# Mixing-matrix products in 64 by 64 tiles of TensorE, and the steps of the kernel in a new order

## The chip, the core and the metric

The kernel runs on one core of one Trainium2 chip. The metric is device microseconds of one execution; a time is the median of several runs. The engines of the core work from queues of their own, in order, and wait for each other through semaphores: PE (TensorE, matrix products), DVE (VectorE), ACT (ScalarE), POOL (GpSimd) and SP (SyncE, which here only issues transfers). Sixteen DMA engines carry what POOL, SP and ACT issue.

## What is computed

Eight batches, each with eight heads, 576 rows and a head size of 64. A small packed query `p` (32 rows a head) attends to `k`, `v`; the result is key and value for the attention of `q`. Then a mixing block works on the heads side by side (512 columns).

```python
def sm_attn(qq, kk, vv):
    s = scale * np.matmul(qq, kk.transpose(0, 1, 3, 2))
    a = np.exp(s - np.max(s, axis=-1, keepdims=True))
    a = a / (np.sum(a, axis=-1, keepdims=True) + 1e-09)
    return np.matmul(a, vv)

p_packed = sm_attn(p, k, v)
x = sm_attn(q, p_packed, p_packed)      # heads put side by side: (8, 576, 512)

wq, wk = x @ w_q, x @ w_k               # (8, 576, 64)
W_tok = scale * np.einsum('bsd,btd->bst', wq, wk)
mixed = np.einsum('bst,btd->bsd', W_tok, x)
out = np.maximum(mixed, 0.0) @ w_out
```

Inputs and output are 32-bit floats, 9.4 MB for each of `q`, `k`, `v` and the output. The products are made in bf16.

## The kernel before

**Steps and their order.** Nothing is planned at run time. The text `ORDER` (lines 13 to 55) lists 521 steps, and the loop at line 600 issues them one by one. `S2.7.1=0,1` is step S2 of batch 7, part 1, into PSUM banks 0 and 1; `@A`, `@V`, `@P` name ACT, DVE or POOL. Each engine takes its own steps in the order of this text, so the text fixes the order within every queue; between engines only data and buffers decide.

**The products, by batch, and the tile of the TensorE array that each uses.** A matmul on R rows and C columns of the array is called R by C here.

- S1 (line 280): packed query times keys, 32 by 32 tiles. X1, TE: exponential on ACT, transposition on DVE.
- PV (313): weights times values, 64 by 64, four tiles of the array in turn. RC, PP, PT: division and transposition on DVE.
- QK (334): 64 by 64; QKE and QD put its result into SBUF.
- S2 (371): scores of `q` against the packed keys, 64 by 128. It needs PT and QV (the transposition of `q`, DVE line 235). X2 is its exponential (ACT), RS and RR the row sums and their reciprocals (DVE), AM the scaling (POOL or DVE, line 403).
- AT (412, 417), WKQ (439, 444), GM (465): 128 by 128. AE, WE, GE take them out of PSUM.
- Y (475): 64 by 64. YE takes it out and scales it.
- **MX (490) and MR (496)**: the product of the small matrix y (weights) with the transposed query side `wkq` (moving). MX makes 512 moving columns at a time, MR the 64 left over from the last chunk. RL, RLF and RLR are the relu on their results.
- OT (538) and OH (578): the relu's result times `w_out`, 128 by 128, 512 columns. OE, OEF, OEH copy it out of PSUM, and ST, STF, STH store it.

WARM (617) are products on a constant that keep TensorE at work early on.

In MX, the loop over `c` picks the half of the rows of the array, `h = halves(c ^ i)`, and bank `c` of two. One matmul has 64 rows, all 128 columns and 512 moving elements. MR has the same weights, over `i` and `h`, with 64 moving elements.

**Transfers.** All loads are issued by POOL's queue: `k`, `v`, `q` of a batch into four buffers each, cast from 32 bits to bf16 on the way (576 KB in SBUF for each; `v` in two halves; `q` of batch 7 in two halves, `LD.q7` and `LD.r7`). Stores go from SP, a few from POOL (`ST.0.8`, `ST.1.4`, `ST.1.8`) and one from ACT. The first step of SP after the start is `HOLD.v7` (line 572): a tiny copy that reads the buffer of `v` of batch 7, so SP's stores wait until that load has landed. SP then issues its stores in order, and a store whose data isn't ready holds up those behind it.

Of the kernel before, what the change touches and what calls it, by code (L numbers as in the profile page):

```python
# [23 lines left out]
PV.2.1 RL.0.1@A RS.1.2@V RS.1.1@V MR.0=2,3 RC.2@V RR.1.2@V AM.1.2@P RR.1.1@V WARM.5=0 PP.2.1@V MX.0.0=0,1 AM.1.1@P
PP.2.0@V PT.2@V AT.1.2=4 LD.k4 AT.1.0=5 RL.0.0@A QK.2=6 RLR.0@A QV.2.2@V AT.1.1=7 AE.1.0@V QKE.2@V S2.2.2=0,1
AE.1.2@A AE.1.1@A QD.1@P X2.2.2@A S2.2.3=2,3 WKQ.1.2=4,5 WKQ.1.1 WKQ.1.0 OT.0.2=6,7 X2.2.3@A WE.1.0@A QD.2@P LD.q3
LD.v4 WE.1.1@V GM.1=0 RS.2.4@V KT.3.2@V RR.2.4@V GE.1@A OT.0.3 Y.1=2,3 YE.1@A OT.0.0=4,5 AM.2.2@V OE.0.1@A
S1.3=0,1,2,3 OT.0.1 X1.3.0@A MX.1.0=6,7 MX.1.1=0,1 AM.2.3@V X1.3.1@A AT.2.3=2 AT.2.2=3 OE.0.0@A TE.3.0@V RL.1.1@A
RL.1.0@A TE.3.1@V AE.2.3@V PV.3.0=4,5 AE.2.2@V PV.3.1 MR.1=2,3 WKQ.2.0=0,1 WKQ.2.1 WKQ.2.2 RC.3@V WE.2.2@A KT.4.2@V
RLR.1@A PP.3.0@V OT.1.2=6,7 PP.3.1@V OT.1.3 OE.1.1@A PT.3@V S1.4=0,1,2,3 OT.1.0=4,5 LD.q4 X1.4.1@A LD.k5 QV.3.2@V  # L30
X1.4.0@A GM.2=6 S2.3.3=2,3 LD.v5 GE.2@V X2.3.3@A TE.4.1@V S2.3.2=6,7 X2.3.2@A LD.q5 Y.2=0,1 OT.1.1 YE.2@V OE.1.0@A
MX.2.0=0,1 RL.2.0@A TE.4.0@V RS.3.4@V MX.2.1=2,3 RL.2.1@A PV.4.0=6,7 RR.3.4@V PV.4.1 QK.3=4 OT.1.4=5 RC.4@V
PP.4.1@V PP.4.0@V OEF.1.4@A QV.4.2@V AM.3.3@P OT.2.0=0,1 PT.4@V QKE.3@A OT.2.1 AT.3.3=2 AM.3.2@P QD.3@P LD.k6
AT.3.2=3 OE.2.0@A AE.3.3@V S2.4.2=6,7 S2.4.3=4,5 X2.4.2@A AE.3.2@A KT.5.2@V QK.4=0 QKE.4@V WKQ.3.1=6,7 WKQ.3.0
WKQ.3.2 LD.v6 X2.4.3@A WE.3.2@A RS.4.4@V S1.5=2,3,4,5 X1.5.1@A X1.5.0@A LD.q6 OT.2.2=0,1 GM.3=6 OT.2.3 QD.4@P
TE.5.1@V GE.3@V MR.2=4,5 TE.5.0@V Y.3=2,3 RR.4.4@V RLR.2@V PV.5.0=6,7 OE.2.1@A PV.5.1 LD.k7 AM.4.3@P YE.3@V
MR.3=4,5 RC.5@V PP.5.1@V RLR.3@A MX.3.1=2,3 RL.3.1@A AM.4.2@P MX.3.0=0,1 OT.3.4=4 RL.3.0@A AT.4.3=5 PP.5.0@V PT.5@V
AT.4.2=2 QV.5.2@V QK.5=3 S2.5.2=6,7 OEF.3.4@A AE.4.3@V AE.4.2@A S2.5.3=0,1 LD.q7 QKE.5@A LD.v7 X2.5.2@A KT.6.2@V
WKQ.4.2=4,5 WKQ.4.0 WKQ.4.1 WE.4.2@V OT.3.0=2,3 X2.5.3@A S1.6=6,7,0,1 X1.6.1@A HA.5@P GM.4=4 X1.6.0@A QD.5@P GE.4@V
OT.3.1 Y.4=4,5 TE.6.1@V LD.r7 YE.4@A RS.5.4@V TE.6.0@V RR.5.4@V OT.3.2=0,1 MX.4.0=6,7 MX.4.1=4,5 OE.3.0@A QV.6.2@V  # L40
PV.6.0=2,3 HOLD.v7 AM.5.3@P AM.5.2@P PV.6.1 OT.3.3 RL.4.0@A RL.4.1@A RC.6@V PP.6.0@V PP.6.1@V ST.0.8@P OE.3.1@A
OT.4.0=6,7 MR.4=4,5 RLR.4@A PT.6@V S2.6.3=2,3 S2.6.2=0,1 X2.6.3@A AT.5.2=4 AT.5.3=5 KT.7.2@V OT.4.1 AE.5.3@V
AE.5.2@A X2.6.2@A ST.1.4@P OE.4.0@A RS.6.4@V RR.6.4@V WKQ.5.2=2,3 WKQ.5.1 WKQ.5.0 AM.6.3@P S1.7=0,1,4,5 WE.5.2@A
# [5 lines left out]
OT.5.1 ST.1.8@P RR.7.0@V OT.5.2=4,5 RR.7.1@V AM.7.2@P ST.5.4 ST.4.1 AM.7.0@V QD.7@P RL.6.1@A RL.6.0@A AT.7.2=6
ST.3.1 AT.7.0=7 AM.7.1@V AE.7.0@V OE.5.0@A AT.7.1=0 AE.7.2@V OT.5.3 WKQ.7.2=6,7 AE.7.1@V WKQ.7.0 WE.7.0@V WKQ.7.1  # L50
OT.6.0=2,3 OE.5.1@A WE.7.1@A GM.7=0 GE.7@V OT.6.1 ST.4.0 Y.7=4,5 OT.6.2=6,7 ST.5.0 YE.7@V MX.7.1=0,1 OE.6.0@A
OEF.6.2@A MX.7.0=4,5 MR.7=2,3 RLF.7.0.1@V RLF.7.0.0@A ST.3.0 ST.5.1 RLF.7.1.1@V OT.6.3 RLF.7.1.0@A OT.7.1=4
OEF.6.3@A OEF.7.1@A OT.7.2=0 OT.7.0=1 RLR.7@A STF.6.2 OH.7.0=2 ST.6.0 OEF.7.2@A STF.6.3 STF.7.1 OEF.7.0@A OT.7.4=3
# [5 lines left out]
def kernel(  # L59
# [426 lines left out]
    def MX(b, i, eng, bk):  # L486
        ps = T["mx", b, i] = bank(bk, [C, 512])
        for c in range(C):
            h = halves(c ^ i)
            nc.tensor.matmul(ps[:, c], T["y", b][h, i], T["wkq", b][h, :, 128:384], start=True, stop=True)  # L490

    def MR(b, eng, bk):
        ps = T["mr", b] = ps_all[:, bk[0]:bk[1] + 1, 0:2 * GR].rearrange("a c (i g) -> a c i g", g=GR)
        for i in range(2):
            for h in range(2):
                nc.tensor.matmul(ps[:, h, i], T["y", b][halves(h), i], T["wkq", b][halves(h), 1, 384:NW],
                                 start=True, stop=True)
# [153 lines left out]
```

## Time and profile before

| | |
|---|---|
| time, median of 3 runs | 104.42 us (104.15 to 104.46) |
| time of the profiled execution | 104.16 us |
| its span (first to last instruction of the program) | 102.3 us |
| PE, DVE, ACT, POOL busy | 91%, 71%, 64%, 47% of the span |
| granted TensorE clock | 1.0 of full speed throughout |
| read from HBM, written to it | 30.15 MB, 9.44 MB |
| issues of SP, POOL, ACT that store results | 18, 3, 1 |

Between the span and the time of the same execution lie 1.86 us that the program's instructions don't cover. Rows of a timeline show the start in us from the beginning of the span, the length, engine, line, operation, output and inputs, sizes and count; in square brackets the idle time before and what ended it. Rows that merge several matmuls give the first start and the time to the last end; an end is modelled and lies some 0.2 us behind the last start, so for the pace of TensorE starts are compared with starts. SPq and POOLq are the queues of SP and POOL.

### The profile page before, as it was taken

To read this page: it belongs to the slowest core of one execution; us is meant where nothing else is said; L and a number is where in the kernel's file an instruction comes from. 1 tells how busy PE (TensorE), PEld (TensorE's weight loads), DVE (VectorE), ACT (ScalarE), POOL (GpSimd) and SP (SyncE) were. 2 spreads that over 40 slices of the span, in tenths; PEclk is the share of its full clock that TensorE was granted. 3 is DMA by queue.
4 is the path that set the end of the run, shared out by engine and by line. 5 is a ranking of instruction groups with operands and counts; after the bars stand their busy time and mean duration, and the time that the engine had idled before them with its cause. 6 is when DMAs were issued, how large, how long until landed. Compare 5 with 4: busy or idle time off the path is not lost.

```text
span 102.3 us, 3572 instructions
## 1 busy us (share of the span) xinstructions
PE 93.1 (91%) x1524; PEld 56.5 (55%) x1540; DVE 72.6 (71%) x145; ACT 65.1 (64%) x109; POOL 48.2 (47%) x78
## 2 busy tenths in 40 slices
...
DMA  1899999999999999999999999999999999998991
GB/s 11 243 225 210 212 213 211 207 210 214 203 214 203 216 206 211 211 213 207 213 214 205 210 213 205 215 212 207 207 267 395 415 425 377 407 415 344 395 382 62
DMA packets 13279, 25.13 MB, mean 246 GB/s; under 512 B 1040, under 2 KB 6416, under 8 KB 13008
## 3 DMA queue, kind: packets, MB, share of 16 engines
...
q8 instruction: 12, 0.20, 0.7%
...
HBM read 30.15 MB, written 9.44 MB: 387 GB/s over the span
## 4 chain that ended last, share of the span: by engine, by line
PE 60%; DMA 23%; DVE 7%; issue 3%; POOL 2%; ACT 1%; DVEq 0%; POOLq 0%
PE ps L538 24%; DMA q_sb<-in_q_dram 23%; PE ps L617 13%; PE ps L313 4%; PE ps L371 3%; PE ps L490 3%; PE ps L417 2%; DVE qT L235 2%; PE ps L444 2%; POOL a L403 2%; PE ps L280 2%; PE ps L465 2%; PE ps L439 2%; PE ps L334 1%; DVE kT L235 1%
## 5 line engine op out<-in xcount | busy, mean ns | idle before, releaser
L538 PE MATMUL ps<-wout,relu 128*128 128x512 bf16 x112 | 29.3, 380 | 0.8 <-issue 0.3
L403 POOL TENSOR_TENSOR a<-e,rr 128x256 bf16<-128x256 f32 (+2 forms) x15 | 15.9, 1071 | 25.2 <-DVE rr L397 16.3
L617 PE MATMUL ps<-o 128*128 128x128 f32 (+3 forms) x80 | 22.6, 432 | 1.3 <-DVE o L133 1.2
L126 ACT ACTIVATE o<-ps 128x1024 f32<-128x1024 f32 (+2 forms) x19 | 16.6, 873 | 5.9 <-PE ps L538 4.4
L538 PEld LDWEIGHTS <-relu 128*128 128x128 bf16 x124 | 10.5, 98 | 11.2 <-issue 1.2
L617 PEld LDWEIGHTS ps<-o 128*128 128x128 f32 x80 | 13.2, 230 | 6.1 <-issue 3.9
L501 ACT ACTIVATE relu<-ps 128x1024 bf16<-128x1024 f32 (+1 forms) x15 | 13.9, 971 | 1.5 <-PE ps L490 1.5
L291 ACT ACTIVATE e1T<-ps 128x576 bf16<-128x576 f32 x16 | 9.6, 649 | 7.5 <-PE ps L280 6.9
L235 DVE STREAM_TRANSPOSE kT<-k_sb 128x1152 uint32<-128x1152 uint32 (+1 forms) x9 | 11.2, 1243 | 2.4 <-DMA k_sb<-in_k_dram 2.4
L376 ACT ACTIVATE e<-ps 128x256 f32<-128x256 f32 (+2 forms) x19 | 11.2, 631 | 2.1 <-PE ps L371 1.9
L392 DVE TENSOR_REDUCE rs<-e 128x16 f32<-128x512 f32 (+2 forms) x13 | 11.0, 854 | 1.8 <-ACT e L376 1.8
L235 DVE STREAM_TRANSPOSE qT<-q_sb 128x1152 uint32<-128x1152 uint32 (+1 forms) x10 | 11.1, 1115 | 1.2 <-DMA q_sb<-in_q_dram 1.1
L171 POOL DMA_DIRECT2D v_sb<-in_v_dram x16 | 10.0, 629 | 3.3 <-PE ps L280 1.4
L235 DVE STREAM_TRANSPOSE e<-e1T 128x288 uint32<-128x288 uint32 x16 | 7.3, 465 | 2.3 <-ACT e1T L291 2.1
L313 PE MATMUL ps<-v_sb,e 64*64 64x192 bf16 x288 | 7.8, 245 | 0.3 <-ACT o L126 0.2
L313 PEld LDWEIGHTS <-e 64*64 64x64 bf16 x288 | 6.0, 107 | 2.7 <-DVE e L235 1.4
L444 PE MATMUL ps<-aT,pqk 128*128 128x256 bf16 (+1 forms) x48 | 7.1, 246 | 0.0
L371 PE MATMUL ps<-ppT,qT 64*128 64x64 bf16 x320 | 6.5, 190 | 0.5 <-DVE qT L235 0.3
L371 PEld LDWEIGHTS <-qT 64*128 64x128 bf16 x320 | 5.5, 94 | 2.6 <-DVE qT L235 2.3
L439 PE MATMUL ps<-pqk,aT 128*128 128x64 bf16 x80 | 5.9, 194 | 0.2 <-ACT aT L126 0.2
L130 DVE COPY aT<-ps 128x1024 bf16<-128x1024 bf16 (+1 forms) x9 | 5.0, 553 | 1.2 <-PE ps L417 1.2
L439 PEld LDWEIGHTS <-aT 128*128 128x128 bf16 x80 | 4.7, 98 | 1.7 <-ACT aT L126 0.6
...
## 6 DMA issues: line engine op xcount, KB each, us to landing
...
```

The source lines that it names most:

```text
L126: nc.scalar.activation(o, i, COPY)
L171: nc.gpsimd.dma_start(v_bufs[b % NL][halves(i), 0:7:2], src)
L235: nc.vector.transpose(o, i)
L313: nc.tensor.matmul(T["pv", b][halves(cc), i], lhsT, rhs, start=n == 0, stop=n == R - 1, skip_group_check=True)
L371: nc.tensor.matmul(ps[:, y, t - t0, i], lhsT, rhs, start=e == 0, stop=e == 1)
L376: nc.scalar.activation(e2[:, t0:t1].rearrange("a t (i y n) -> a y (t i) n", i=2, y=2), T["s2", b, c].rearrange("a y t i n -> a y (t i) n") ...
L392: nc.vector.tensor_reduce(rs[:, t0 * H:t1 * H], src, axis=AX, op=ADD)
L403: e.tensor_tensor(a2[:, t0:t1].rearrange("a t i (u l) -> a (t i u) l", l=L), e2v(b, c), T["rr", b][:, t0 * H:t1 * H].to_broadcast((P, (t1 ...
L439: nc.tensor.matmul(o, aT[:, i, t * P:(t + 1) * P], pqk[:, i, 0:Dl], start=i == 0, stop=i == 1)
L501: nc.scalar.activation(o, i, RELU)
L538: nc.tensor.matmul(ps, lhsT, wout[:, j, :], start=j == 0, stop=j == NJ - 1)
L617: nc.tensor.matmul(bank(int(bk), [w]), warm[:, 0:P], rhs, start=True, stop=True)
```

## The change

MX and MR are written with one more loop, over the two halves `z` of the weights' columns. Each matmul becomes two, with 64 columns of weights each, that write to the lower and the upper half of PSUM's partitions. MX has 64 matmuls in place of 32, MR 64 in place of 32.

```diff
     def MX(b, i, eng, bk):
         ps = T["mx", b, i] = bank(bk, [C, 512])
         for c in range(C):
             h = halves(c ^ i)
-            nc.tensor.matmul(ps[:, c], T["y", b][h, i], T["wkq", b][h, :, 128:384], start=True, stop=True)
+            for z in range(2):
+                nc.tensor.matmul(ps[halves(z), c], T["y", b][h, i, halves(z)], T["wkq", b][h, :, 128:384],
+                                 start=True, stop=True)
 
     def MR(b, eng, bk):
         ps = T["mr", b] = ps_all[:, bk[0]:bk[1] + 1, 0:2 * GR].rearrange("a c (i g) -> a c i g", g=GR)
         for i in range(2):
             for h in range(2):
-                nc.tensor.matmul(ps[:, h, i], T["y", b][halves(h), i], T["wkq", b][halves(h), 1, 384:NW],
-                                 start=True, stop=True)
+                for z in range(2):
+                    nc.tensor.matmul(ps[halves(z), h, i], T["y", b][halves(h), i, halves(z)],
+                                     T["wkq", b][halves(h), 1, 384:NW], start=True, stop=True)
```

`ORDER` has the same 521 steps; up to `LD.q2 WKQ.0.1` (in its seventh line) it is unchanged, and behind that the steps stand in another order, 34 of them on another engine. Of the text, the part around the second half of batch 7:

```diff
...
-QD.6@P PP.7.1@V MX.5.0=6,7 RL.5.0@A WKQ.6.2=2,3 PT.7@V WKQ.6.0 WKQ.6.1 WE.6.2@A MX.5.1=4,5 S2.7.1=0,1 OT.5.4=6
-X2.7.1@A GM.6=7 S2.7.2=2,3 RL.5.1@V ST.3.4 GE.6@A X2.7.2@A S2.7.0=0,1 Y.6=4,5 QK.7=7 YE.6@A RS.7.1@V QKE.7@A
...
+AM.6.2@P GE.5@V AT.6.3=0 AT.6.2=1 AE.6.3@V Y.5=6,7 OE.4.1@A PV.7.0=2,3 QV.7.0@V AE.6.2@A YE.5@A PV.7.1 MR.5=4,5
+MX.5.1=0,1 RLR.5@A RC.7@V RL.5.1@A MX.5.0=6,7 WKQ.6.1=4,5 RL.5.0@A WKQ.6.0 WKQ.6.2 PP.7.0@V PP.7.1@V ST.3.0
+OT.5.4=2 PT.7@V S2.7.2=0,1 S2.7.1=6,7 ST.0.8@P WE.6.2@V S2.7.0=4,5 X2.7.2@A RS.7.2@V GM.6=3 GE.6@V OT.5.0=0,1
+OT.5.1 OEF.5.4@A X2.7.0@A RR.7.2@V RS.7.0@V X2.7.1@A Y.6=2,3 RS.7.1@V AM.7.2@P RR.7.0@V AM.7.0@V YE.6@A AT.7.2=4
...
```

What the new text means for the queues, from batch 1 on, read out of it:

```
POOL before: LD.q2 LD.O LD.k3 LD.v3 AM.1.0 AM.1.2 AM.1.1 LD.k4 QD.1 QD.2 LD.q3 LD.v4 LD.q4 LD.k5 LD.v5 LD.q5
             AM.3.3 AM.3.2 QD.3 LD.k6 LD.v6 LD.q6 QD.4 LD.k7 AM.4.3 AM.4.2 LD.q7 LD.v7 HA.5 QD.5 LD.r7
             AM.5.3 AM.5.2 ST.0.8 ST.1.4 AM.6.3 AM.6.2 QD.6 ST.1.8 AM.7.2 QD.7
POOL after:  LD.q2 LD.O LD.k3 LD.v3 LD.k4 AM.1.1 AM.1.2 AM.1.0 QD.1 LD.q3 LD.v4 AM.2.2 AM.2.3 LD.q4 LD.k5 QD.2
             LD.v5 LD.q5 LD.k6 AM.3.3 LD.v6 QD.3 LD.q6 AM.4.2 LD.k7 AM.4.3 LD.v7 LD.q7 QD.4 ST.1.4 HA.5 QD.5
             AM.5.3 AM.5.2 LD.r7 QD.6 AM.6.3 AM.6.2 ST.0.8 AM.7.2 QD.7 ST.1.8
SP before:   HOLD.v7 ST.3.4 ST.2.1 ST.2.0 ST.5.4 ST.4.1 ST.3.1 ST.4.0 ST.5.0 ST.3.0 ST.5.1
             STF.6.2 ST.6.0 STF.6.3 STF.7.1 STF.7.2 STF.7.0 STH.7.0 ST.7.4
SP after:    HOLD.v7 ST.3.0 ST.3.4 ST.2.1 ST.2.0 ST.4.0 ST.5.4 ST.3.1 ST.4.1 ST.5.0 ST.5.1
             ST.6.0 STF.6.2 STF.6.3 ST.7.4 STF.7.1 STF.7.0 STF.7.2 STH.7.0
```

On PE, going through the steps in order and counting every place where the tile shape (32 by 32, 64 by 64, 64 by 128, 128 by 128) differs from that of the step before: 83 places before and 70 after; of these 38 and 33 up to the start of `S2.3.3`, 44 and 36 behind it, one at it. (The old order with the new tiles would have 80, the new order with the old tiles 84.) The last steps on PE are `OT.7.4 OH.7.1` before and `OH.7.1 OH.7.0` after.

More of the change, by code (lines that the diff above doesn't have):

```diff
@@ L24 @@
[L24 to L43, printed above, removed]
@@ L49 @@
[L49 to L53, printed above, removed]
@@ new lines @@
+OE.0.0@A MX.1.0=4,5 AE.2.3@V AE.2.2@A PV.3.0=6,7 LD.v5 MR.1=2,3 PV.3.1 RLR.1@A MX.1.1=0,1 WKQ.2.2=2,3 RL.1.0@V
+RL.1.1@A LD.q5 RC.3@V LD.k6 PP.3.1@V WKQ.2.1 WKQ.2.0 KT.4.2@V PP.3.0@V OT.1.2=4,5 WE.2.2@A OT.1.3 S1.4=0,1,2,3
+OE.1.1@A X1.4.1@A OT.1.0=6,7 PT.3@V X1.4.0@A QV.3.2@V GM.2=4 S2.3.3=2,3 GE.2@V X2.3.3@A TE.4.1@V S2.3.2=0,1 Y.2=4,5
+OT.1.1 YE.2@V X2.3.2@A TE.4.0@V RS.3.4@V MX.2.0=4,5 PV.4.0=2,3 PV.4.1 OE.1.0@A RL.2.0@A RR.3.4@V QK.3=0 RC.4@V
+MX.2.1=6,7 PP.4.1@V OT.1.4=1 PP.4.0@V AM.3.3@P RL.2.1@A OT.2.0=4,5 PT.4@V OT.2.1 AT.3.3=2 QKE.3@A QV.4.2@V
@@ new lines @@
+OEF.1.4@A S2.4.3=6,7 OE.2.0@A X2.4.3@A S2.4.2=0,1 AM.3.2@V LD.v6 QD.3@P AE.3.3@V AT.3.2=3 AE.3.2@A LD.q6 KT.5.2@V
+X2.4.2@A WKQ.3.0=4,5 RS.4.4@V WKQ.3.1 WKQ.3.2 S1.5=6,7,2,3 WE.3.2@A X1.5.0@A OT.2.2=0,1 X1.5.1@A GM.3=4 RR.4.4@V
+AM.4.2@P GE.3@A OT.2.3 Y.3=6,7 TE.5.1@V QK.4=2 TE.5.0@V YE.3@V PV.5.0=4,5 MR.3=6,7 PV.5.1 OE.2.1@A QKE.4@V LD.k7
+AM.4.3@P LD.v7 LD.q7 QV.5.2@V RC.5@V RLR.3@A MR.2=0,1 RLR.2@A MX.3.0=2,3 QD.4@P PP.5.0@V MX.3.1=6,7 OT.3.4=0
+AT.4.3=1 PP.5.1@V PT.5@V AT.4.2=4 RL.3.0@A S2.5.3=2,3 RL.3.1@A OEF.3.4@A S2.5.2=6,7 QK.5=5 AE.4.2@V AE.4.3@V
@@ new lines @@
+WKQ.4.0=0,1 KT.6.2@V WKQ.4.2 QKE.5@V X2.5.3@A WKQ.4.1 OT.3.0=2,3 X2.5.2@A S1.6=6,7,4,5 ST.1.4@P HA.5@P OT.3.1
+QD.5@P X1.6.0@A X1.6.1@A WE.4.2@V RS.5.4@V TE.6.0@V TE.6.1@V GM.4=0 GE.4@A OT.3.2=6,7 HOLD.v7 Y.4=4,5 PV.6.0=0,1
+OE.3.0@A YE.4@A RR.5.4@V PV.6.1 QV.6.2@V MX.4.0=2,3 RC.6@V RL.4.0@A PP.6.1@V AM.5.3@P PP.6.0@V MX.4.1=4,5 RL.4.1@A
+OT.3.3 MR.4=2,3 AT.5.3=0 AM.5.2@P PT.6@V RLR.4@V AT.5.2=1 KT.7.2@V AE.5.2@A S2.6.2=4,5 S2.6.3=2,3 X2.6.2@A QK.6=1
+AE.5.3@V OT.4.0=4,5 X2.6.3@A LD.r7 QKE.6@A RS.6.4@V OE.3.1@A OT.4.1 QD.6@P S1.7=2,3,0,1 OE.4.0@A RR.6.4@V
```

24 lines of the change are left out of this document (16 added, 8 removed).

## The prediction

> **What bounds the kernel now.** I read the page first: shares, slices, and the chain of work that ended last.
>
> ```profile
> span 102.3 us, 3572 instructions
> PE 93.1 (91%) x1524; PEld 56.5 (55%) x1540; DVE 72.6 (71%) x145; ACT 65.1 (64%) x109; POOL 48.2 (47%) x78
> ...
> DMA  1899999999999999999999999999999999998991
> GB/s 11 243 225 210 212 213 211 207 210 214 203 214 203 216 206 211 211 213 207 213 214 205 210 213 205 215 212 207 207 267 395 415 425 377 407 415 344 395 382 62
> ...
> PE 60%; DMA 23%; DVE 7%; issue 3%; POOL 2%; ACT 1%; DVEq 0%; POOLq 0%
> ```
>
> Two things are full at once. TensorE is busy 91% of the span, and the DMA engines show 9 in every slice but two from the second on. The rate has two levels: about 210 GB/s while loads run (they write half of what they read, 32 bits to bf16), and about 400 from slice 30 (76 us) on, when stores run. The chain names PE for 60%, but a chain follows one thread. So I ask where PE waits for data, and whether the DMA engines have anything left to give. First the chain of waits in order of time, then PE's timeline at the same place:
>
> ```profile
> 34.56 11.71 DMA q_sb<-in_q_dram
> ...
> 46.29 1.39 DVE qT L235
> ...
> 47.73 0.78 PE L371 MATMUL ps<-ppT,qT 64*128 64x64 bf16 x40 [0.26 <-DVE qT L235]
> ```
>
> `q` of batch 3 lands at 34.56+11.71 = 46.27, DVE transposes it, and S2.3, for which PE stood idle 0.26 us, begins at 47.73. Up to there PE follows the loads, and time saved on it only lengthens this wait. From there on PE runs behind the loads.
>
> The end of the run, from the busy time in chosen stretches (PE, PEld, DVE, ACT, POOL, then clock, DMA share, GB/s) and SP's queue:
>
> ```profile
> 78.00:80.00 2.00, 2.00 (x50) 1.43 (x43) 1.96 (x6) 1.77 (x5) 1.33 (x3) 1.00 0.96 379
> 85.00:87.00 2.00, 2.00 (x19) 1.17 (x18) 1.54 (x4) 2.00 (x3) 0.01 (x1) 1.00 0.93 370
> 91.00:93.00 2.00, 2.00 (x15) 0.81 (x16) 0.87 (x2) 1.87 (x3) 0.00 (x0) 1.00 1.04 416
> 93.00:95.00 2.00, 2.00 (x11) 0.89 (x10) 0.84 (x2) 1.73 (x5) 0.00 (x0) 1.00 0.84 323
> ```
>
> ```profile
> 76.36 0.60 SPq L572 DMA_DIRECT2D touch<-v_sb  x1
> 77.00 0.58 SPq L557 DMA_DIRECT2D out_dram<-orem  x1
> 77.63 1.51 SPq L561 DMA_DIRECT2D out_dram<-o  x2
> 83.41 0.34 SPq L557 DMA_DIRECT2D out_dram<-orem  x1
> 83.85 6.37 SPq L561 DMA_DIRECT2D out_dram<-o  x6
> 92.61 0.54 SPq L592 DMA_DIRECT2D out_dram<-o  x1
> ...
> 98.37 0.34 SPq L557 DMA_DIRECT2D out_dram<-orem  x1
> ```
>
> With 416 GB/s as the full rate, the stretches at 78, 85 and 93 us lack 0.18, 0.22 and 0.45 us of transfer, 0.85 us in all: (416-379)/416 x 2 and so on. The largest hole, at 93, lies behind SP's pause between 90.2 and 92.61. All else in the tail is full. So whatever PE saves, the end can come forward by about 0.85 us and no more, unless the bytes change, which they don't.
>
> **The change part by part.** *Tile shapes.* What does a change of shape cost? PE's timeline:
>
> ```profile
> 49.59 0.61 PE L490 MATMUL ps<-wkq,y 64*128 64x512 bf16 x4
> 50.12 0.94 PE L313 MATMUL ps<-v_sb,e 64*64 64x192 bf16 x36
> 50.90 0.39 PE L334 MATMUL ps<-wqk,ppT 64*64 64x128 bf16 x8
> ...
> 90.91 1.04 PE L538 MATMUL ps<-wout,relu 128*128 128x512 bf16 x4
> 91.88 0.61 PE L490 MATMUL ps<-wkq,y 64*128 64x512 bf16 x4
> 92.32 0.22 PE L496 MATMUL ps<-wkq,y 64*128 64x64 bf16 x4
> 92.48 3.63 PE L538 MATMUL ps<-wout,relu 128*128 128x512 bf16 x16
> 95.94 0.81 PE L578 MATMUL ps<-wout,relu 128*128 128x384 bf16 x4
> ```
>
> OT's sixteen take 95.94-92.48 = 3.46 us from start to start, 0.216 for 512 columns. MX's four, followed by MR in the same shape, take 92.32-91.88 = 0.44: two rounds of 0.216, two matmuls side by side in each. Followed by PV in another shape, they take 50.12-49.59 = 0.53. The change of shape costs 0.53-0.43 = 0.10 us; between OT and MX it is 0.97-4x0.216 = 0.11. I take 0.10. Behind S2.3.3 the steps change shape 36 times in place of 44: 8 x 0.10 = **0.8 us less on PE**. The five fewer ahead of it lie in front of the wait for `q` and are costed at nothing: that wait hides them, and if it were gone they would give 0.5 more.
>
> *MX itself.* Eight matmuls in place of four for a batch, in two rounds of four tiles. The trace has no 64 by 64 matmul of 512 columns. From below: PV runs four such tiles at once, 36 matmuls in 50.90-50.12 = 0.78 us, of which nine rounds of 192 columns at OT's pace would be 0.73. So MX stays at 0.43: nothing. From above: if the two halves that read the same moving rows ran one after the other, MX would take 0.86, 0.43 more, for six batches (2 to 7) behind S2.3 2.6 us. I take the lower end, PV's row being nearest: same tiles, same type. *MR*: between the 0.06 of now (0.16 from 92.32 to 92.48, less a change of shape) and the 0.18 or so of QK's four rounds (0.39 less the last matmul's 0.2), 0 to 0.7 us for six batches; I take 0, since MR's matmuls have half of QK's columns and its rounds four tiles. *Weight loads*: from the groups of instructions by form,
>
> ```profile
> L490 PEld LDWEIGHTS <-y 64*128 64x128 bf16 x32 | 1.2, 94 | 2.0 <-DVE y L484 0.8 <-issue 0.6 <-ACT y L482 0.4
> L313 PEld LDWEIGHTS <-e 64*64 64x64 bf16 x288 | 6.0, 107 | 2.7 <-DVE e L235 1.4 <-issue 0.4 <-DVE rr L397 0.4
> ...
> L501 ACT ACTIVATE relu<-ps 128x1024 bf16<-128x1024 f32 x13 | 12.8, 1029 | 1.5 <-PE ps L490 1.5
> L503 DVE TENSOR_SCALAR relu<-ps 128x1024 bf16<-128x1024 f32 x1 | 1.2, 1226 | 0.4 <-PE ps L490 0.4
> ...
> L403 POOL TENSOR_TENSOR a<-e,rr 128x1024 bf16<-128x1024 f32 x4 | 7.6, 1904 | 13.9 <-DVE rec L317 7.5 <-DVE rr L397 5.0 <-PE ps L490 1.4
> ```
>
> a load of 64 columns takes 107 ns, longer than one of 128 (94). The 64 loads more lie under the matmuls, as PV's do at full pace: nothing. Uncovered, the eight loads more of a batch would be 0.86 us, 5 us for six batches; PV's pace with a load for every matmul excludes that. The Trainium skill, "TensorEngine Tiling (Array Packing)", Restrictions, speaks against the change here: column tiling switches the fast weight load off. The two durations agree with it; by that rule the loads cost 128 x 107 - 64 x 94 ns = 7.7 us of loading, and by PV's pace none of it shows.
>
> *Engines and the queues of POOL and DVE.* 34 steps change engine, nearly all between ACT and DVE; the longest, a relu of 1024 columns, takes 1.03 us on ACT and 1.23 on DVE, and neither engine is full (64%, 71%). Near the end, OE.5.1 and OE.6.0 go to DVE, which is busy 0.87 of 2 us from 91 to 93. AM.2.2 and AM.2.3 go to POOL, ahead of `LD.q4` and `LD.k5`. POOL's loads have the 11.71 us from issue to landing of the first row above as cover, since several stand in line; the 1.9 us of the larger of them on POOL cost nothing. Without that cover every us late is a us of idle DMA. `LD.k4` and `LD.k6` go earlier, and the order of loads up to `k7` stays.
>
> *SP and the last loads.* Here is the price I do see. Loads come one after another: DVE starts on `q6` at 69.14 and on `k7` at 71.97, both having waited for the landing, so 2.8 us for a full load and 1.4 for half of one. SP's copy at 76.36 marks `v7`'s landing (71.95+1.4+2.8 = 76.2).
>
> ```profile
> 69.14 1.38 DVE L235 STREAM_TRANSPOSE qT<-q_sb 128x1152 uint32<-128x1152 uint32 x1 [0.50 <-DMA q_sb<-in_q_dram]
> 71.97 1.42 DVE L235 STREAM_TRANSPOSE kT<-k_sb 128x1152 uint32<-128x1152 uint32 x1 [0.40 <-DMA k_sb<-in_k_dram]
> ...
> 78.18 0.77 DVE L235 STREAM_TRANSPOSE qT<-q_sb 128x576 uint32<-128x576 uint32 x1
> 79.45 0.15 DVE L317 RECIPROCAL rec<-ps 128x2 f32<-128x2 f32 x1
> 79.64 0.61 DVE L321 SCALAR_TENSOR_TENSOR pp<-ps,rec,mask 128x128 bf16<-128x128 f32 x2
> 80.28 0.31 DVE L235 STREAM_TRANSPOSE ppT<-pp 128x128 uint32<-128x128 uint32 x1
> 80.69 0.40 PE L371 MATMUL ps<-ppT,qT 64*128 64x64 bf16 x16
> ```
>
> Now `v7` is loaded ahead of `q7`, lands at 74.8, and frees SP 1.5 us earlier, while `q7` (76.2), `ST.1.4` (256 KB, 0.6 us: 76.8) and `r7` (78.2) are still to come on POOL's queue. SP's first store, issued at 75.4, has its packets under way by some 77.4: the shortest transfer of the output takes 2.8 us from issue to landing,
>
> ```profile
> DMA to landing us min/median/max: 2.8/5.0/9.6
> ```
>
> of which 0.6 us carries its 256 KB. The last 0.8 us of `r7` then shares the engines and takes 1.6: `r7` at 79.0. QV.7.0 now stands ahead of RC.7, PP.7 and PT.7 on DVE: 0.77+0.15+0.61+0.31 = 1.84, so S2.7 can begin at 80.9 to 81.0. PE would be there at 80.69-0.8+0.87 = 80.8 (OT.5.4, four times 0.216, now comes first). The stall is **0.2 us**, between 0 (no sharing) and 1.2 (sharing from 76.4 on).
>
> *Stores at the end.* `ST.1.8` (1 MB, 2.5 us of transfer) goes from the middle to the end of POOL's queue, behind QD.7, and `ST.3.0` and `ST.4.0` move ahead of the store on which SP waited until 83.41. Both put transfers where holes were (85 and 93 us). PE's last product is followed by a copy of 384 columns in place of 512, 0.1 us shorter, within what I leave uncertain.
>
> *Sum.* 0.8 on PE, less 0.2 at S2.7: 0.6 us, under the 0.85 that the DMA engines allow. Against the execution's own 104.16 that is 103.56; the median of the runs shown lies 0.26 higher, so **103.8 us** on its scale.
>
> **The rivals.**
>
> *Nothing comes out.* The end belongs to the transfers as much as to PE; if the holes of 0.85 us only move (SP waits behind ST.5.4 or ST.5.1 again), the last store lands when it did: 104.4. For it: DMA at 9 throughout. Against: the new order of the stores. The same time follows if the 0.10 us isn't due to the shape but to any change from one step's operands to another's, so that the change doesn't do what it says; MX to MR at 0.44 without it speaks against that.
>
> *Slower: the last load is late.* SP's stores, let go before `q7` and `r7` are in, take half of the engines from 76.4 on (I assume equal shares of two queues); ST.1.4 and `r7` need 1.8 us alone and 3.6 shared, `r7` lands at 80.0, and S2.7 starts at 81.9 to 82.0, 1.2 late. Then 104.42-0.8+1.2 = 104.8; with `q7` caught too or two stores beside each load, 105.2. It decides from a landing of 79.7 on, at which 0.8 are lost. For it: SP's hold is released earlier. Against: issue of the first store at 75.4 needs time to bear. The Trainium skill, "DMA: Bandwidth & Descriptors", Arbitration, has each DMA engine take turns between queues packet by packet; no row of the run before shows it, loads and stores hardly overlapping there.
>
> *Slower: pairs of tiles on the same rows don't overlap.* MX doubles: 104.42-0.6+2.6 = 106.4. PV's and Y's rows speak against it.
>
> **How the numbers follow.** Forecast 0.48, with 103.3 (0.85, the 0.1 of the shorter last copy and half of the 0.26 between profiled time and median) to 104.1 as its own range; no gain 0.20; the late load 0.27; doubled MX 0.05. A measurement of this kernel tells 0.3%, 0.3 us, from no change, so faster means under 104.1: 0.48; within: 0.20; slower: 0.32. The range runs from 103.2 (the same with the whole 0.26) to 105.2 (the late load's far end) and leaves out doubled MX and some of each end.
>
> **What would show it.** MX from start to start at 0.43 for eight matmuls; a change of shape still at 0.10, and 36 of them behind S2.3; S2.3 at 47.7 as before; S2.7 near 81; PE's last product 0.5 to 0.8 us earlier; no stretch under 0.95 of DMA share between 84 and 96. Wrong would be: S2.7 at 82 or later, a slice of DMA under 9 while loads run, or MX at 0.86.

## The result, and the profile after

| | before | changed |
|---|---|---|
| median, 22 runs each | 104.75 us | 105.35 us |
| ratio to before | 1 | 1.0057 (95%: 1.0034 to 1.0081) |
| profiled execution, its span | 104.16, 102.3 us | 104.83, 103.1 us |

The change makes the kernel 0.6 us slower. Runs more than 1.5% above the fastest of the same kernel are left out of every ratio in this document: one of the changed kernel's 22, one each of f1 and h1 below, and five of i2's 12. The forecast was 103.8 us, faster; that was wrong. The median lies just above the range's end of 105.2; on the scale of the prediction's own 104.42 it is 104.42 x 1.0057 = 105.0. From the page of the changed kernel:

```profile
span 103.1 us, 3725 instructions
...
PE 94.7 (92%) x1604; PEld 57.1 (55%) x1604; DVE 75.3 (73%) x147; ACT 62.9 (61%) x106; POOL 50.3 (49%) x79
...
DMA  2999999999999999999999999999989999998974
GB/s 20 236 229 210 213 210 209 210 210 213 206 209 209 210 208 214 210 210 211 209 211 207 217 209 203 216 211 206 226 206 388 402 412 402 393 413 355 366 294 162
...
q8 instruction: 12, 0.20, 0.7%
...
PE 59%; DMA 16%; POOL 7%; ACT 6%; issue 5%; DVE 4%; ACTq 0%; POOLq 0%
```

PE is busy 1.6 us longer, though it has fewer changes of shape to make. The DMA row has an 8 in slice 30 (75 to 77 us), where before has a 9. In the chain of work the share named "issue" has grown from 3% to 5%: time in which PE waited for nothing that the profile shows. PE's timeline, in which the number in square brackets is the idle time ahead of a row:

```profile
48.19 0.78 PE L371 MATMUL ps<-ppT,qT 64*128 64x64 bf16 x40 [0.50 <-ACT e1T L291]
...
50.05 0.41 PE L491 MATMUL ps<-wkq,y 64*64 64x512 bf16 x4
50.29 0.91 PE L313 MATMUL ps<-v_sb,e 64*64 64x192 bf16 x36
...
56.28 0.38 PE L444 MATMUL ps<-aT,pqk 128*128 128x256 bf16 x2
56.96 0.23 PE L439 MATMUL ps<-pqk,aT 128*128 128x64 bf16 x2 [0.29 <-ACT aT L126]
...
64.43 0.29 PE L439 MATMUL ps<-pqk,aT 128*128 128x64 bf16 x4
64.79 0.39 PE L444 MATMUL ps<-aT,pqk 128*128 128x256 bf16 x2
...
66.43 0.48 PE L280 MATMUL ps<-kT,pT 32*32 32x288 bf16 x31
67.09 0.28 PE L280 MATMUL ps<-kT,pT 32*32 32x288 bf16 x1 [0.18 <-issue]
...
70.24 0.60 PE L491 MATMUL ps<-wkq,y 64*64 64x512 bf16 x8
70.78 1.04 PE L541 MATMUL ps<-wout,relu 128*128 128x512 bf16 x4
...
93.47 0.23 PE L499 MATMUL ps<-wkq,y 64*64 64x64 bf16 x8
93.53 0.39 PE L491 MATMUL ps<-wkq,y 64*64 64x512 bf16 x4
```

The tiles do what they were priced at. Four of the new matmuls followed by PV, now in the same shape, take 50.29-50.05 = 0.24; eight with a change of shape behind them take 70.78-70.24 = 0.54, which is 0.44 and 0.10. MR's eight take 0.06. But PE waits in new places: 56.96, 64.79 and 67.09.

To see all of these, I took each matmul's start, less the start before it, less its predecessor's columns at OT's pace, less 0.095 us where the shape changes. What is left is the time lost. Behind S2.3.3, losses over 0.06 us, in us (gaps of 0.216 in OT, which are missing records, are taken off):

```
before   52.60 .08   54.51 .12   56.77 .16   61.33 .12   62.99 .07   65.95 .09   74.01 .16                 sum 0.80
changed  53.07 .19   55.80 .07   56.96 .46   60.21 .19   61.17 .10   61.90 .11   64.79 .24   67.09 .35
         72.67 .12   79.40 .12   81.13 .15   83.33 .08                                                     sum 2.17
```

That is 1.37 us more. S2.3 begins 48.19-47.73 = 0.46 later, and eight changes of shape fewer save 0.76: 1.07 in sum. PE's last matmul starts at 98.89 in place of 97.62, 1.27 later; the other 0.2 isn't attributed. Most of the new loss lies between 53 and 67 us.

The same stretches of the tail as before, with 76 to 78 us added; first the changed kernel, then two rows of before that aren't shown yet:

```profile
76.00:78.00 2.00, 2.00 (x33) 1.31 (x23) 1.79 (x4) 2.00 (x4) 1.15 (x1) 1.00 0.82 224
78.00:80.00 2.00, 2.00 (x48) 1.52 (x49) 1.18 (x3) 1.89 (x5) 1.95 (x3) 1.00 1.03 396
...
85.00:87.00 2.00, 2.00 (x15) 0.67 (x12) 1.96 (x5) 1.02 (x3) 0.35 (x1) 1.00 0.98 388
91.00:93.00 2.00, 2.00 (x28) 0.84 (x24) 1.47 (x2) 0.90 (x3) 0.00 (x0) 1.00 1.03 424
93.00:95.00 2.00, 2.00 (x24) 0.86 (x23) 1.60 (x4) 1.48 (x5) 0.00 (x0) 1.00 0.87 346
...
97.00:99.00 2.00, 2.00 (x15) 1.00 (x12) 0.98 (x2) 0.84 (x2) 0.00 (x0) 1.00 0.88 330
```

```profile
76.00:78.00 2.00, 2.00 (x48) 1.25 (x45) 1.58 (x5) 1.12 (x3) 2.00 (x2) 1.00 1.10 398
...
97.00:99.00 2.00, 0.84 (x7) 0.40 (x5) 1.10 (x2) 0.28 (x1) 0.00 (x0) 1.00 1.02 381
```

Two differences. At 76 to 78 us, the turn from loads to stores, the DMA share falls to 0.82, from 1.10: a hole. And it is 0.88 in place of 1.02 at 97 to 99 us, where PE is still at work in the changed kernel and the transfers wait for its results. (The 0.87 at 93 us is no difference: before had 0.84 there.) The queue rows suggest where the hole comes from, first POOL's issues of before, then those of POOL and SP in the changed kernel in order of time:

```profile
66.83 0.59 POOL L177 DMA_DIRECT2D q_sb<-in_q_dram  x1
...
71.23 0.66 POOL L559 DMA_DIRECT2D out_dram<-o  x1
71.88 0.58 POOL L557 DMA_DIRECT2D out_dram<-orem  x1
```

```profile
71.64 0.59 POOL L177 DMA_DIRECT2D q_sb<-in_q_dram  x1
...
75.30 0.60 SPq L575 DMA_DIRECT2D touch<-v_sb  x1
76.02 0.64 SPq L564 DMA_DIRECT2D out_dram<-o  x1
...
79.29 0.66 POOL L562 DMA_DIRECT2D out_dram<-o  x1
```

Before, POOL issued the store `ST.0.8` (1 MB) at 71.23, behind the last load `r7`. It stood in line behind the loads and ran as soon as they were done, while SP's stores, held until `v7` was in, only started. In the new order `ST.0.8` stands behind AM.6.2 and is issued at 79.29.

So there are two suspects for 0.6 us: PE's lateness, and the hole. The tiles are a third.

### The profile page after: what moved, and what is told of

Its sections match the earlier page's. It is cut to its first block, busy times and chain, and to the rows that moved or that the text cites. A ratio compares the mean times of both kernels' runs of the same rounds, so it can differ in the third digit from the quotient of the medians.

```text
span 103.1 us, 3725 instructions
## 1 busy us (share of the span) xinstructions
PE 94.7 (92%) x1604; PEld 57.1 (55%) x1604; DVE 75.3 (73%) x147; ACT 62.9 (61%) x106; POOL 50.3 (49%) x79
## 4 chain that ended last, share of the span: by engine, by line
PE 59%; DMA 16%; POOL 7%; ACT 6%; issue 5%; DVE 4%; ACTq 0%; POOLq 0%
PE ps L541 24%; DMA k_sb<-in_k_dram 16%; PE ps L620 13%; PE ps L313 4%; PE ps L371 3%; POOL a L403 3%; PE ps L444 3%; PE ps L491 2%; ACT e1T L291 2%; PE ps L280 2%; PE ps L417 2%; PE ps L439 2%; ACT relu L504 1%; DVE kT L235 1%; POOL v_sb L171 1%
## 5 line engine op out<-in xcount | busy, mean ns | idle before, releaser
L541 PE MATMUL ps<-wout,relu 128*128 128x512 bf16 x124 | 30.8, 380 | 0.0
L403 POOL TENSOR_TENSOR a<-e,rr 128x256 bf16<-128x256 f32 (+2 forms) x16 | 17.8, 1127 | 21.5 <-ACT e L376 7.5
L126 ACT ACTIVATE o<-ps 128x1024 f32<-128x1024 f32 (+1 forms) x15 | 13.6, 911 | 4.6 <-PE ps L541 4.5
L504 ACT ACTIVATE relu<-ps 128x1024 bf16<-128x1024 f32 (+1 forms) x14 | 13.2, 993 | 1.4 <-PE ps L491 1.4
L174 POOL DMA_DIRECT2D k_sb<-in_k_dram x7 | 5.1, 728 | 5.5 <-DMA q_sb<-in_q_dram 5.5
L130 DVE COPY o<-ps 128x1024 f32<-128x1024 f32 (+3 forms) x5 | 4.0, 796 | 3.2 <-PE ps L541 2.4
```

The costliest lines, as they stand in the source:

```text
L126: nc.scalar.activation(o, i, COPY)
L403: e.tensor_tensor(a2[:, t0:t1].rearrange("a t i (u l) -> a (t i u) l", l=L), e2v(b, c), T["rr", b][:, t0 * H:t1 * H].to_broadcast((P, (t1 ...
L504: nc.scalar.activation(o, i, RELU)
L541: nc.tensor.matmul(ps, lhsT, wout[:, j, :], start=j == 0, stop=j == NJ - 1)
```

## Experiments

Each ratio is to the kernel of before on the same chip, with a 95% interval. "Turn" is the time in which DMA engines stood empty between 74 and 82 us, worked out from the records of the transfers in steps of 0.25 us; it is 0.00 before and 0.40 us in the changed kernel. "PE" is the start of the last matmul. Both are of one profiled execution, which can lie far from the median: those of e2, e4, f3, g1 and h3 were the longest of their kernels, that of e1 the shortest of its 12. So a place on PE is best compared with the end of the same execution, as is done under "How much PE has to spare".

### The tiles and the order apart

```diff
 e1: ORDER as before; MX and MR as changed
 e2: ORDER as changed; MX and MR as before
 e3: ORDER of before up to S2.3, the new one behind; new tiles
 e4: ORDER of before up to S1.6, the new one behind; new tiles
```

> The steps in the order of the kernel before, MX and MR in 64 by 64 tiles as in the changed kernel. Theory A (the loss is the new order's: PE waits that the old order did not have, some 1.3 us behind S2.3 and 0.5 us ahead of it): this is no slower than before, 0 to 0.3 us faster, since behind S2.3 the shape changes 41 times in place of 44; ratio 0.997 to 1.001. Rival B (the 64 by 64 products cost what the traces do not show): the whole loss stays, ratio 1.005 to 1.008.

> The new order, MX and MR in 64 by 128 tiles as before. Theory A: the waits of the new order stay and the shape changes 45 times behind S2.3 in place of 36, 0.9 us more at 0.1 us each; slower than the changed kernel, ratio to before 1.010 to 1.015. Rival B: the loss goes with the tiles, ratio 0.998 to 1.002.

> New tiles; old order up to the scores of batch 3 (S2.3 at some 48 us), new order behind that. Theory A: the 0.5 us by which S2.3 began late in the changed kernel go if the order ahead of it made them, ratio 1.000 to 1.003; if q of batch 3 merely landed late in that one execution, the ratio stays at the changed kernel's 1.005 to 1.008.

> New tiles; old order up to the S1 products of batch 6 (some 65 us), new order behind that. Theory A with the loss at S2.3 and between there and S1.6, where the changed kernel fell from 0.46 to 0.97 us behind: ratio 0.996 to 1.001. If the loss is in the last third (the changed kernel fell back another 0.4 us there, and its last stores come 0.7 us later): ratio 1.003 to 1.008.

| | ratio | PE, us | turn, us |
|---|---|---|---|
| before | 1 | 97.62 | 0.00 |
| changed | 1.0057 (1.0034 to 1.0081) | 98.89 | 0.40 |
| e1 | 1.0031 (0.9999 to 1.0064) | 98.38 | 0.02 |
| e2 | 1.0084 (1.0056 to 1.0112) | 98.80 | 1.12 |
| e3 | 1.0078 (1.0049 to 1.0106) | 99.61 | 0.48 |
| e4 | 1.0189 (1.0154 to 1.0225) | 100.03 | 2.37 |

The new order alone costs 0.8%. The tiles bring nothing in the old order. e4 is the surprise: with only the last third in the new order it is the slowest of these, and its hole is the widest. The stretches of e4:

```profile
76.00:78.00 2.00, 2.00 (x53) 1.14 (x51) 1.97 (x4) 2.00 (x3) 0.28 (x1) 1.00 0.65 134
78.00:80.00 2.00, 2.00 (x20) 1.05 (x18) 1.15 (x3) 1.88 (x4) 2.00 (x2) 1.00 0.18 56
```

### PE's instructions

In e1 PE also lost time for which no releaser is shown ("issue"), 0.2 and 0.5 us. The trace shows transfers of 16 KB on the queue of instructions, one some 6 us after the other in the middle of the kernel. Behind 45 us, the profiles of nine kernels (the changed one, e1, e3, e4, f1, g1, g2, h1, h2) show twelve idle stretches of PE of 0.18 us or more that are marked "issue". All twelve ended 2.2 to 2.6 us after the start of such a transfer. Some of them, with smaller losses for which no releaser is shown:

```
kernel    start of transfer -> PE goes on (lost there)
changed   58.76 -> 61.17 (.10)    64.79 -> 67.09 (.35)
e1        58.10 -> 60.46 (.20)    64.13 -> 66.38 (.50)
e4        54.22 -> 56.54 (.26)    60.19 -> 62.46 (.83)
before    71.68 -> 74.01 (.16)    59.03, 65.38: none lost this way
```

At most of these places PE runs through many short matmuls (S1, PV, MR). To move the transfers against the steps, 64 products of two columns, whose results nobody uses, were put at the beginning (128 instructions with their weight loads), in place of three early products on the constant:

```diff
-WARM.22.128=0
+WARM.19.128=0 TINY.64=4
+            elif f[0] == "TINY":
+                for n in range(int(f[1])):
+                    x, y = n % 4, n // 4 % 4
+                    z = aT_bufs[0][quarter(x), 0, 512:544]
+                    nc.tensor.matmul(ps_all[quarter(y), int(bk) + x, 0:2], z, z[:, 0:2], start=True, stop=True)
 f1: in before; f2: in e1; f3: in the changed kernel
```

> The kernel before with 64 tiny products (32 by 32 tiles, two columns, results unused) put in early, at some 9 us, in place of 3 of the 22 narrow warm-up products: 122 more instructions on PE, as many as the new tiles bring, but ahead of the dense part. Theory F (PE ran dry of instructions in the kernels with new tiles: idle PE that nothing releases, 0.2 to 0.8 us about 2.3 us behind the start of a 16 KB instruction transfer): if it depends on where a transfer's end falls in the stream, idle stretches of this kind show up here too, 0.2 to 0.8 us, ratio 1.002 to 1.008. If only the density of instructions counts, none show, ratio 0.999 to 1.001.

> Old order, new tiles, and the same 64 tiny early products. Theory F by place in the stream: the transfers fall half a piece elsewhere, the idle stretches of 0.20 and 0.50 us at 60 and 66 us vanish or move; if they vanish, ratio 0.995 to 0.999. By density: they stay, ratio 1.001 to 1.006. Rival (they are accidents of one execution): no rule.

> The changed kernel with the 64 tiny early products. Theory F by place: idle PE without a releaser (0.10 us at 61 and 0.35 us at 67) vanishes or moves; the waits of the new order (AE.3.2, QD.4, TE.5) stay; ratio 1.000 to 1.004 if it vanishes. By density: as the changed kernel, 1.004 to 1.008.

f1: 0.9977 (0.9949 to 1.0005), f2: 1.0028 (1.0000 to 1.0056), f3: 1.0122 (1.0086 to 1.0157). The idle time moved as the theory has it: f2 had no idle stretch of this kind left, and f1, with the old tiles and the old order, now had one (transfer at 57.95). PE's timeline of f1:

```profile
59.67 0.25 PE L313 MATMUL ps<-v_sb,e 64*64 64x192 bf16 x4
60.36 0.86 PE L313 MATMUL ps<-v_sb,e 64*64 64x192 bf16 x32 [0.43 <-issue]
```

But the times didn't follow: f2 was expected at 0.995 to 0.999 without them. f1 lost 0.6 us on PE there, its last matmul started 0.7 later than before (98.31), and its time is not longer. So a loss of that size on PE doesn't reach the end of f1. f3 is slower than the changed kernel with PE earlier (98.29): its hole at the turn is 1.09 us.

### Mending the new waits

Two of the waits have names. At 56.96 PE waited for AE.3.2, which ACT issued behind an exponential of 1024 columns; AM.3.2, on which it depends, had moved from POOL to DVE. At 64.79 it waited for QD.4, which the new order puts on POOL behind `LD.v7` and `LD.q7`, as the changed kernel's POOL rows show (the copy of `pqk` is QD.4):

```profile
62.59 1.29 POOL L171 DMA_DIRECT2D v_sb<-in_v_dram  x2
63.86 0.57 POOL L177 DMA_DIRECT2D q_sb<-in_q_dram  x1
64.41 0.32 POOL L128 COPY pqk<-pqk 128x128 bf16<-128x128 bf16 x1
```

f4 puts these steps back to about where before had them:

```diff
 f4: the changed ORDER, with
-QD.4@P behind LD.q7                +QD.4@P ahead of LD.v7
-AM.3.2@V AT.3.2 AE.3.2 behind S2.4 +AM.3.2@P AT.3.2 AE.3.2 ahead of it
-RR.4.4 AM.4.2 ahead of GE.3        +RR.4.4 AM.4.2 behind TE.5.0
```

> The changed kernel with six steps moved back towards the old order: QD.4 ahead of the loads of v7 and q7 on POOL; AM.3.2 on POOL and AT.3.2, AE.3.2 ahead of the scores of batch 4; RR.4.4 and AM.4.2 behind TE.5.0. Theory A (the new order's waits): the waits of 0.46 us on AE.3.2, 0.24 us on QD.4 and 0.19 us on TE.5.0 go, 0.9 us in all; ratio 0.997 to 1.001. If other steps are late in their place, the ratio stays at 1.004 to 1.008.

f4: 1.0058 (1.0035 to 1.0081), nothing gained. The two named waits went, and two on POOL took their place; PE in f4:

```profile
56.34 0.39 PE L444 MATMUL ps<-aT,pqk 128*128 128x256 bf16 x2 [0.37 <-POOL pqk L128]
...
63.85 0.56 PE L417 MATMUL ps<-idb,a 128*128 128x128 bf16 x7 [0.72 <-POOL a L403]
```

QD.3 now stood behind AM.3.2 as well as the load of `v6` on POOL. AM.4.2, waiting for the RR.4.4 that was moved back, began at 60.53 in place of 59.39, and AM.4.3 behind it and `LD.k7` ended just before 63.85. The wait at 60.21, for TE.5, stayed. In f4 the waits moved, they didn't vanish. So no run won time back by taking a named wait away.

### The hole at the turn

```diff
 g1: the changed ORDER;  g2: f3;  g3: f4;  in each
-ST.0.8@P behind AM.6.2             +ST.0.8@P directly behind LD.r7
 g4: the ORDER of before, with
-ST.0.8@P ahead of ST.1.4           +ST.0.8@P behind AM.6.2
```

> The changed kernel with one step moved: ST.0.8 (1 MB stored by POOL) directly behind the last load LD.r7 on POOL, where the old order had it, in place of behind AM.6.2. Theory D (the end is set by the DMA engines, and the new order leaves them idle between the last loads and the first stores, 0.40 us at 76 to 78 us in the changed kernel and 1.0 to 2.4 us in others with its tail): no idle share left at 74 to 80 us; at least 0.3 us faster than the changed kernel, ratio to before 1.000 to 1.003. Theory A (PE waits of the new order): PE's last product stays at 98.9 and the ratio at 1.004 to 1.008.

> The same move of ST.0.8 in the changed kernel with 64 early tiny products (1.0122, idle DMA of 1.1 us at 76 to 82 us, though PE's last product began at 98.3, 0.6 us earlier than in the changed kernel). Theory D: the hole of 1.1 us goes and the time with it, ratio 0.999 to 1.004. Theory A: 1.010 to 1.015 as it was.

> The same move of ST.0.8 together with the six steps moved back for PE's waits (1.0058 without it). Theory D: ratio 1.000 to 1.003, like the changed kernel with the move alone. Theory A: as without it, 1.004 to 1.008.

> The kernel before with ST.0.8 moved the other way, behind AM.6.2 on POOL, where the new order has it; nothing else. Theory D: the DMA engines stand idle 0.5 to 1.2 us between 76 and 80 us, and the end comes 0.3 to 0.9 us later, ratio 1.003 to 1.009. Theory A: PE is untouched, ratio 0.999 to 1.001.

| | ratio | of the same without it | PE, us | turn, us |
|---|---|---|---|---|
| g1 | 1.0062 (1.0036 to 1.0087) | 1.0057 | 99.62 | 0.00, from 0.40 |
| g2 | 1.0052 (1.0028 to 1.0076) | 1.0122 | 99.00 | 0.00, from 1.09 |
| g3 | 1.0066 (1.0041 to 1.0091) | 1.0058 | 99.39 | 0.00, from 0.43 |
| g4 | 1.0192 (1.0153 to 1.0231) | 1 | 97.41 | 2.2, from 0.00 |

One store, moved down by some 35 steps of the old order, costs 1.9% (g4), with PE as early as ever. Its stretches:

```profile
76.00:78.00 2.00, 2.00 (x49) 1.19 (x46) 1.61 (x6) 1.16 (x4) 2.00 (x2) 1.00 0.38 117
78.00:80.00 2.00, 2.00 (x47) 1.54 (x48) 1.97 (x6) 1.76 (x4) 1.74 (x4) 1.00 0.54 199
...
95.00:97.00 2.00, 1.95 (x11) 0.98 (x10) 0.36 (x1) 1.26 (x3) 0.00 (x0) 1.00 1.03 401
97.00:99.00 2.00, 0.63 (x6) 0.30 (x4) 0.89 (x2) 0.28 (x1) 0.00 (x0) 1.00 1.01 388
99.00:101.00 2.00, 0.00 (x0) 0.00 (x0) 0.00 (x0) 0.00 (x0) 0.00 (x0) 1.00 1.01 368
```

PE is done at 97.6, and the engines carry stores at full share behind it: what was lost at the turn is missing here. A hole of 1 to 2 us decides the end (f3 against g2, g4). The 0.4 us of the changed kernel doesn't: filling it gains nothing (g1 and g3, for which 1.000 to 1.003 was expected). In these two and in the changed kernel the program ends 4.17 to 4.19 us behind the start of PE's last matmul, with the hole or without it: there the stores wait for PE anyway. What filling the hole would bring if PE were on time isn't shown: in g1's profiled execution PE stood idle 0.29 and 0.43 us without a releaser, at 61.73 and 67.65, and its last matmul started 0.73 us later than the changed kernel's.

### How much PE has to spare

In h3 and h4 nothing changes but PE's time: four extra products on the constant (two in h4), whose results nobody uses, ahead of GM.4 in the kernel of before. And the two halves of the new order are tried by themselves.

```diff
 h1: e4 with ST.0.8@P directly behind LD.r7
 h2: the new ORDER up to S1.6, that of before behind it; new tiles
 h3: the ORDER of before
-HA.5@P GM.4=4
+HA.5@P WARM.5=4 GM.4=4
 h4: the same with WARM.2=4
```

> The order of before up to S1.6, the new one behind it (as in e4), with ST.0.8 directly behind LD.r7. Theory (the hole at the turn from loads to stores made the 1.9% of e4, and the new tail by itself costs nothing): the hole is closed to under 0.3 us and the ratio is 1.000 to 1.004, if MX.7.0 begins by 93.0 us. Rival (the new tail itself costs, by its waits or by the order of its stores): 1.006 or more with the hole closed.

> The new order up to S1.6 and the order of before behind it, new tiles throughout. Theory (PE is made late in the middle, S1.6 0.97 us behind, by the new order's waits): the last product is late by about 1 us, of which some 0.7 is slack, ratio 1.002 to 1.006. Rival (the last third makes the loss): 0.998 to 1.001.

> The kernel of before with 4 extra early products whose results nobody uses (about 1.3 us of PE time) ahead of GM.4, behind the middle of the kernel. Theory (before ends by its stores and PE has about 0.7 us to spare there): about 0.6 us reach the end, ratio 1.004 to 1.008. Rival (PE sets the end one to one): 1.012. Rival (PE has more to spare than that): 1.000.

> The same with about half the extra PE time (some 0.6 us). Theory (0.7 us to spare): 0.998 to 1.003. Rival (one to one): 1.006.

| | ratio | time longer, us | PE later, one execution, us | its end later, us | last matmul to end, us |
|---|---|---|---|---|---|
| before | 1 | 0 | 0 | 0 | 4.71 |
| h4 | 1.0018 (0.9992 to 1.0044) | 0.2 (-0.1 to 0.5) | 0.44 | 0.38 | 4.65 |
| h3 | 1.0064 (1.0027 to 1.0102) | 0.7 (0.3 to 1.1) | 1.07 | 1.90 | 5.55 |
| changed | 1.0057 (1.0034 to 1.0081) | 0.6 (0.4 to 0.8) | 1.27 | 0.72 | 4.17 |
| h2 | 1.0072 (1.0044 to 1.0100) | 0.75 (0.5 to 1.0) | 1.79 | 1.13 | 4.06 |
| h1 | 1.0024 (0.9995 to 1.0054) | 0.25 (-0.1 to 0.6) | 1.82 | 1.29 | 4.18 |

"Time longer" is the ratio less 1, times 104.4. The last three columns are of the profiled executions, against that of before: the end is that of the span, and the last one is the time from the start of the last matmul to it.

That last column tells who sets the end. With the new last third it is 4.16 to 4.19 us in seven kernels (the changed one, e3, f4, g1, g2, g3, h1), however late PE is; with the old one it is 4.00, 4.07 and 4.06 in e1, f1 and h2. There the end follows PE. (f2's 4.52 and h4's 4.65 lie nearer to before's.) In before it is 4.71: PE's last product came 0.5 to 0.7 us before it would have set the end. That is the slack. f1's last matmul started 0.68 later than before's and e1's 0.76, and their spans ended 0.04 and 0.05 later; the changed kernel's started 1.27 later and its span ended 0.72 later, so about 0.5 was absorbed. Where the column is far longer, transfers set the end: 7.25 in g4, 5.88 in f3, 5.29 in e4, 5.24 in e2, all with holes at the turn.

The doses alone don't show the slack: the intervals of h3 and h4 allow all of their 1.07 and 0.44 us at the end. And h3's profiled execution isn't typical, 106.02 us with a median of 105.02; in it the end came 1.90 later, more than PE did. Its stretches show how a late PE can cost more than its own lateness. The late products make results late, SP's queue waits for them until 84.48 (before until 83.41), the DMA engines are half empty at 85 to 87 us, and from 91 us on everything is full, to a later end:

```profile
85.00:87.00 2.00, 2.00 (x16) 0.83 (x15) 1.75 (x6) 1.81 (x4) 0.84 (x2) 1.00 0.54 202
91.00:93.00 2.00, 2.00 (x14) 0.68 (x14) 0.72 (x2) 1.02 (x1) 0.00 (x0) 1.00 1.02 401
...
97.00:99.00 2.00, 1.85 (x12) 0.99 (x11) 0.84 (x2) 0.66 (x2) 0.00 (x0) 1.00 1.00 379
```

h2 has the changed kernel's loss with the last third of before and no hole (turn 0.03): the loss is made up to S1.6. h1 has the new last third without its hole, and from e4's 1.0189 it comes down to 1.0024: the new tail by itself costs nothing that this run can tell. h1's profiled execution was a long one (105.40 us, its median is 104.76), with 0.46 and 0.84 us lost in stretches marked "issue", which are most of its late PE. PE in it; a transfer on the queue of instructions began at 59.53:

```profile
60.96 0.22 PE L499 MATMUL ps<-wkq,y 64*64 64x64 bf16 x2
61.83 0.25 PE L499 MATMUL ps<-wkq,y 64*64 64x64 bf16 x6 [0.65 <-issue]
```

### The tiles alone, once more

e1 and f2 hinted that the tiles cost something in the old order. A third pair, with 32 of the tiny products (in place of 64):

```diff
-WARM.22.128=0
+WARM.19.128=0 TINY.32=4
 i1: in before; i2: in e1
```

> The kernel of before with 32 tiny early products whose results nobody uses, which shift PE's later instructions by about 64 places. Theory (a shift by itself costs at most what PE has to spare): 0.997 to 1.003.

> The order of before with the new tiles (e1) and the same 32 tiny products. Theory (the tiles save 0.4 us of PE behind S2.3, four shape changes, and bring nothing at the end, since PE has time to spare): within 0.2% of i1_old_plus64. Rival (the new tiles cost by themselves, as e1 against before and f2 against f1 hint): 0.3 to 0.5% above i1_old_plus64.

i1: 1.0018 (0.9993 to 1.0044); i2: 1.0045 (1.0008 to 1.0082). The new tiles against the old ones, in the old order, are +0.31% (e1), +0.51% (f2 against f1) and +0.27% (i2 against i1): three times the same sign, on average 0.36%. Only the second is clear of its noise (0.1 to 0.9%), and i2's runs scatter widely (104.42 to 106.33 us), so this is a hint. In the new order it is 1.0057 against 1.0084, -0.27%, with intervals that overlap. There the new tiles save 14 changes of shape (84 to 70), in the old order 3.

## Why the prediction was wrong

*What bounds the kernel.* Half right. PE and the transfers are both full, but the sum used the statement "whatever PE saves, the end can come forward by about 0.85 us" as if PE's time came out at the end one to one up to there. But PE's last product didn't set the end of before's profiled execution: it had 0.5 to 0.7 us to spare, so time saved on PE reaches the end only as far as the stores come earlier with it. e1, which saves PE three changes of shape behind S2.3, gained nothing. Two readings were also short: three slices of the DMA row from the second on are under 9, not two, and by the prediction's own measure 97 to 99 us (381 GB/s) lacks 0.17 us more.

*Tile shapes, MX, MR, weight loads: right as durations.* A change of shape is still 0.10, MX 0.44 for eight matmuls, MR 0.06. The 64-column loads took 106 ns each and are nowhere to be seen in MX's pace. By the Trainium skill, "TensorEngine Tiling (Array Packing)", Key Properties, changing the tiling mode drains TensorE; it gives no figure, and these rows put it at 0.10 us. The size of the saving on PE, 8 x 0.10 = 0.8 us, fits these durations too. It was lost again on the way.

*Engines and the queues of POOL and DVE: the step that failed.* "34 steps change engine ... neither engine is full", and the POOL moves, were costed at nothing, from shares of busy time and from the cover of the loads. That cover is one for transfers; it says nothing of the compute steps in the same queue. Behind S2.3.3 PE lost 2.17 us in place of 0.80. AE.3.2 behind an exponential on ACT, its input moved to DVE (0.46), QD.4 behind two loads on POOL (0.24) and the wait for TE.5 at 60.21 (0.19) make 0.89 of them; 0.45 more, at 61.17 and 67.09, have no releaser and follow transfers of instructions, which the prediction didn't consider. That the order costs time is shown by e2 (0.8% with the old tiles, though there the hole sets the end). That it does so up to S1.6, by way of PE, is shown by h2 against h1 (1.0072 to 1.0024, both without a hole, both with their end some 4.1 us behind the last matmul). That these single waits are the reason is read from the trace; f4, which took two of them away, got others. What such a step is worth can't be read from how busy its engine is on average, only from what stands ahead of it and how long before its use it ends.

*SP and the last loads.* `r7` landed at 79.02 by the records of the transfers, where 79.0 was estimated. The rival of the late load, from 79.7 on, fell with that. S2.7 began at 82.87 and not near 81, which the prediction named as a sign of being wrong, but not for `q`: DVE transposed it without a wait at 80.09, and PE was busy with OT.5.4 until S2.7. PE was late itself. The other sign, a slice of DMA under 9 while loads run, came too: it is the hole at the turn, for which the prediction had no cause.

*Stores at the end.* The move of `ST.1.8` was priced, that of `ST.0.8` was not: it left a hole of 0.40 us at the turn. In the changed kernel this costs nothing that the runs can tell (g1), but the same move costs 1.9% where PE is on time (g4). No price for it was in the sum or the range; that the changed kernel got off with a small hole was luck.

*S2.3 at 47.7.* It began at 48.19. DVE's row says why: `q` of batch 3 landed 0.46 us later than before.

```profile
46.76 1.38 DVE L235 STREAM_TRANSPOSE qT<-q_sb 128x1152 uint32<-128x1152 uint32 x1 [0.59 <-DMA q_sb<-in_q_dram]
...
80.09 0.77 DVE L235 STREAM_TRANSPOSE qT<-q_sb 128x576 uint32<-128x576 uint32 x1
```

Kernels with the old order up to there had S2.3 anywhere from 47.2 to 48.8 in their executions, so nothing suggests that the change did this.

*The sum.* -0.6 us was forecast, +0.6 measured. By the profiled executions: the new waits and instructions +1.4, the changes of shape -0.8, `q` 0.5 and 0.2 unattributed make PE 1.27 late, and less the 0.54 by which the end moved closer to PE's last matmul (4.71 to 4.17) that is 0.7 us, the 0.72 of the spans; the medians say 0.4 to 0.8. The slower side had its chance, 0.32, but through a mechanism that didn't occur.

*What stays open.* That the 16 KB transfers hold PE up is argued from their times and from f1 and f2, where shifting the instructions moved the idle time; no run took the transfers away. Whether the tiles really cost some 0.3% in the old order, and why, isn't settled: lost time for instructions fits e1, but f2 had none. Why the hole is 0.40 us in the changed kernel and 1.09 in f3, with the same order, isn't known. No version beat the kernel of before beyond its interval; f1 comes nearest.
